# A two-layer MLP behind Nystrom attention: a fourth raw-weight buffer, spills issued by GpSimd, and a rearranged prologue

## The chip, the cores and the metric

One core of a Trainium2 chip. The metric is device time in microseconds (us) of one execution. The page and the trace come from one profiled execution, whose span runs from its first to its last instruction. Engines: PE is TensorE (PEld its weight loads), DVE is VectorE, ACT is ScalarE, POOL is GpSimd, SP is the sync engine, whose queue (SPq) issues all DMAs of the kernel before.

## The reference

Attention over 4 batches, 8 heads, 576 positions, head size 64, with 32 landmarks, then two MLP layers (512 to 2048 to 512) over the 2304 tokens:

```python
q_lm = q.reshape(B, H, m, S // m, D).mean(axis=3)
k_lm = k.reshape(B, H, m, S // m, D).mean(axis=3)
A = sm(q, k_lm); Bm = sm(q_lm, k_lm); C = sm(q_lm, k)
Z = Bm.transpose(0, 1, 3, 2) / (norm1(Bm) * norminf(Bm) + 1e-06)
for _ in range(6):
    Z = 2 * Z - Z @ Bm @ Z
x = (A @ Z @ C @ v)          # heads side by side: 2304 x 512
h = x @ w_in;  x = (h - np.tanh(h)) @ w_out          # first MLP
h = x @ w_in2; out = (h * np.tanh(softplus(h))) @ w_out2   # second MLP
```

## The kernel before

Products are made to float32 accuracy by splitting each operand into a high and a low part (`split`, line 98), three matmuls per product. The weights come from memory as 64-bit values; a load (`load_raw`, line 113) brings 512 KB into a buffer of the pool `raw`, and a conversion (`f32_a`, `f32_b`, lines 124 to 154) makes float32 from it: two ScalarE passes (lines 131 and 137) and a VectorE combination (line 144), after which the buffer is free. Output weights are then split (lines 99 and 100). Input weights of the first MLP are kept whole, two loads side by side in one tile of the pool `w1` (four tiles, `keep_job`, line 163), and spilled to memory once (line 171), to be reloaded for each later batch (line 466). `convert` (line 176) runs a list of such jobs with some loads ahead. In the first batch the list is: four loads for the first of four column blocks of the input weights, nine output weights, then the other column blocks and output weights in the order of their due slots.

The work of the first part is divided into slots. A slot is one of 16 blocks of 128 hidden features for one half (288 positions) of one batch, so there are 32 slots a batch and 128 in all. A slot issues the first-layer matmuls (`h1`, lines 500 to 502, two of each line), the activation (`vec`), and, three slots later, the output matmuls (`y1`, lines 603 to 607). The input weights of a column block are folded with the attention's middle matrix first (`p_gen`, line 468: 16 matmuls on line 211, then the split on lines 479 and 481); slots 0 to 3 need block 0, slots 4 to 7 block 1, and so on. AT, the transposed and split A, comes from `attn_a` (line 409) for each half batch. After slot 127 come 96 slots of the second MLP (lines 524 to 526 and 626 to 631).

The attention of a batch is one serial chain (`attn_pre`, line 240): the means over positions (line 246), scaled copies into QB, KB and behind k (lines 251, 253); the scores of the landmarks against k in two halves, two banks each (line 275, its matmuls on line 211), copied and reduced to maxima (lines 279 to 283); exponentials (lines 293, 296); transposes of C (lines 307, 324) with copies (lines 311, 327); norms of B; C v (lines 351 to 360); B B^T (lines 373 to 375, matmuls on line 218); the iterations (lines 381 to 399); the middle matrix Z0 (lines 400 to 404). A generator yields after each part; a slot, or a round of the prologue, takes the next part of each generator, one in its middle and one at its end.

The prologue (lines 733 to 778) runs the first batch's `attn_pre` at raised priority beside the conversions, and the first half batch's `attn_a`, called the early attention here, from round 8. The order on each engine is laid down when the kernel is built, by priority and readiness in a model; each engine then executes its list in order. The shared PSUM pool `ps_m` has two banks, `ps_h` two, and `ps_y` four, which hold the output sums of `y1`. In the second MLP `convert` uses a second pool of two raw buffers besides `raw`, and `raw` also holds outputs on their way out.

Of the kernel before, what the change touches and what calls it, by code (L numbers as in the profile page):

```python
# [8 lines left out]
F32 = mybir.dt.float32  # L9
# [5 lines left out]
ALU = mybir.AluOpType  # L15
AX = mybir.AxisListType
# [11 lines left out]
def kernel(  # L28
# [11 lines left out]
    nc = tc.nc  # L40
    B, NPAIR, _, S = qT.shape
    NG = NPAIR // 2
# [3 lines left out]
    R = S // M  # L46
# [15 lines left out]
    const = ctx.enter_context(tc.tile_pool(name="const", bufs=1))  # L62
    wo_p = ctx.enter_context(tc.tile_pool(name="wo", bufs=NF))
    st_p = ctx.enter_context(tc.tile_pool(name="st", bufs=4))
    raw_p = ctx.enter_context(tc.tile_pool(name="raw", bufs=3))
    ps_y = ctx.enter_context(tc.tile_pool(name="ps_y", bufs=4, space=PSUM))
    ps_h = ctx.enter_context(tc.tile_pool(name="ps_h", bufs=2, space=PSUM))
    ps_m = ctx.enter_context(tc.tile_pool(name="ps_m", bufs=2, space=PSUM))

    w1s = dram.tile([NG, 4, 128, 2, 512], F32, name="w1s")  # L70
# [15 lines left out]
    V = nc.vector  # L86
    A = nc.scalar
    G = nc.gpsimd
# [24 lines left out]
    def load_raw(src, pool=None):  # L113
        raw = (pool or raw_p).tile([128, 512, 2], U32, tag="raw", name="raw")
        nc.sync.dma_start(out=raw.rearrange("p f t -> p (f t)"), in_=src.bitcast(U32))
        return raw
# [7 lines left out]
    def f32_a(raw, on_act):  # L124


        y = st_p.tile([128, 512], F32, tag="y", name="y")
        hi = raw.bitcast(F32)[:, :, 1]
        one = tables["prelu"]
        if one:  # L130
            A.activation(out=y, in_=hi, func=ACTF.Prelu, scale=2.0 ** -112, alpha=2.0 ** 32)
        else:
            A.activation(out=y, in_=hi, func=ACTF.Copy, scale=2.0 ** -112)
        lo = raw[:, :, 0]
        if on_act:

            A.activation(out=lo, in_=raw.bitcast(U16)[:, :, 1], func=ACTF.Copy, scale=2.0 ** -13,
                         bias=2.0 ** -14 - 0.5)
        else:
            V.tensor_scalar(out=lo, in0=lo, scalar1=29, scalar2=None, op0=ALU.logical_shift_right)  # L140
        return y, lo, one

    def f32_b(y, lo, one, t):
        V.scalar_tensor_tensor(
            out=t.bitcast(U32) if one else lo, in0=y.bitcast(U32), scalar=3, in1=lo,
            op0=ALU.logical_shift_left, op1=ALU.bitwise_or,
        )
        yield 0
        if not one:
            V.scalar_tensor_tensor(  # L150
                out=t.bitcast(U32), in0=y.bitcast(U32), scalar=0x80000000, in1=lo,
                op0=ALU.bitwise_and, op1=ALU.bitwise_or,
            )
            yield 0
# [8 lines left out]
    def keep_job(src, g, j, a):  # L163
        def where():
            if a == 0:
                w1t[0, g, j] = w1_p.tile([128, 2, 512], F32, tag="w1", name="w1")
            return w1t[0, g, j][:, a, :]

        def done(y):
            if a == 1:  # L170
                nc.sync.dma_start(out=w1s[g, j], in_=w1t[0, g, j])
                if g:
                    ready.append(j)
        return src, done, where

    def convert(jobs, act_share=1, more=None):
        n = len(jobs)
        raws, st, los = {}, {}, {}
        ahead = 4 if more else 2

        def fetch(i):
            if i < n:
                raws[i] = load_raw(jobs[i][0], more if more and i % 5 > 2 else None)

        for i in range(ahead):
            fetch(i)
        for i in range(n + 2):
            if i < n:
                st[i], *los[i] = f32_a(raws.pop(i), i % act_share == 0)
            if i - 1 in los:  # L190
                where = jobs[i - 1][2]
                yield from f32_b(st[i - 1], *los.pop(i - 1), where() if where else st[i - 1])
            fetch(i + ahead)
            if i >= 2:
                jobs[i - 2][1](st.pop(i - 2))
            yield 1

    ready = []
    w1t = {}
# [7 lines left out]
    def blocks(outs, lhs, rhs):  # L207
        for c in range(4):
            for e in range(2):
                ps = slice(64 * e, 64 * e + 64)  # L210
                mm(outs[e][32 * c:32 * c + 32], lhs[ps, c, :], rhs(ps, c % 2, c // 2), start=True, stop=True,  # L211
                   tile_position=(64 * e, 32 * c))

    def heads(o, lhs, rhs):

        for c in range(4):
            ps = slice(32 * c, 32 * c + 32)
            mm(o[ps], lhs[ps], rhs[ps], start=True, stop=True, tile_position=(32 * c, 32 * c))

    ATt = {}  # L220
    adone = set()
    ZT = {}

    inp = {}

    def attn_load(b, g):
        r = inp[b, g] = {}
        r["q"] = in_p.tile([128, 2, S], F32, tag="q", name="q")
        r["k"] = in_p.tile([128, 2, S + M], F32, tag="k", name="k")
        nc.sync.dma_start(out=r["k"][:, :, 0:S], in_=kT[b, 2 * g:2 * g + 2].rearrange("a p s -> p a s"))  # L230
        nc.sync.dma_start(out=r["q"], in_=qT[b, 2 * g:2 * g + 2].rearrange("a p s -> p a s"))

    def v_load(b, g):
        t = in_p.tile([128, 5, 256], F32, tag="v", name="v")
        inp[b, g]["v"] = t
        cols = slice(256 * g, 256 * g + 256)
        nc.sync.dma_start(out=t[:, 0:4, :], in_=v[b, 0:512, cols].rearrange("(j p) c -> p j c", p=128))
        nc.sync.dma_start(out=t[0:64, 4, :], in_=v[b, 512:S, cols])

    def attn_pre(b):  # L240
        qs = [inp[b, g]["q"] for g in range(NG)]
        ks = [inp[b, g]["k"] for g in range(NG)]
        red = sm_p.tile([128, NG, 2, 2, M], F32, tag="red", name="red", bufs=1)

        def mean(g, x, t):
            V.tensor_reduce(out=red[:, g, x], in_=t[:, :, 0:S].rearrange("p a (m r) -> p a m r", r=R),
                            axis=AX.X, op=ALU.add)

        def scaled(g, x):
            if x == 0:  # L250
# [20 lines left out]
        for hf in range(2):  # L271
            for g in range(NG):
                inp[b, g]["c"] = c[:, g]
            pp = [ps_m.tile([128, 512], F32, tag="m", name="m") for g in range(NG)]
            blocks([p[:, 0:NH] for p in pp], QB, lambda ps, g, a: ks[g][ps, a, NH * hf:NH * hf + NH])
            yield 1
            n = NH - M * hf
            for g, p in enumerate(pp):
                A.activation(out=c[:, g, NH * hf:NH * hf + NH], in_=p[:, 0:NH], func=ACTF.Copy)
                V.tensor_reduce(out=mx[:, g, hf:hf + 1], in_=p[:, 0:n], axis=AX.X, op=ALU.max)  # L280
                yield 0
                if hf:
                    V.tensor_reduce(out=mx[:, g, 3:4], in_=p[:, n:NH], axis=AX.X, op=ALU.max)
                    yield 0
            yield 1
# [31 lines left out]
        bb = sm_p.tile([128, 2, NG, M], F32, tag="bb", name="bb", bufs=1)  # L317
# [30 lines left out]
                        in1=mask.rearrange("p (o a) m -> p o a m", o=1).to_broadcast([128, NG, 4, M]), op=ALU.mult)  # L348
        yield 1

        pv = ps_m.tile([128, 512], F32, tag="m", name="m")
        for g in range(NG):
            for j in range(5):
                n = 128 if j < 4 else 64
# [14 lines left out]
        for g in range(NG):  # L369
            A.activation(out=yv[:, g, 32:96], in_=pv[:, 64 * g:64 * g + 64], func=ACTF.Copy,  # L370
                         scale=n4[:, 2, g:g + 1])
        yield 1
        py = ps_m.tile([128, 512], F32, tag="m", name="m")
        for g in range(NG):
            heads(py[:, 32 * g:32 * g + 32], bb[:, 1, g, :], bb[:, 1, g, :])
        yield 1
        nr = n4.rearrange("p t (g o) -> p t g o", o=1)[:, 3]
        V.tensor_tensor(out=yv[:, :, 0:32], in0=py[:, 0:64].rearrange("p (g n) -> p g n", g=NG),
# [354 lines left out]
    if True:  # L733
# [4 lines left out]
        def w1i_jobs(j):  # L738
            return [keep_job(w1i[j, g, a], g, j, a) for g in range(NG) for a in range(2)]

        def wo_jobs(src, dst, lo, hi):
            return [split_job(src[i], wo_p, "w", dst, i) for i in range(lo, hi)]

        jobs = w1i_jobs(0) + wo_jobs(w1o, W1o, 0, NPRE)
# [6 lines left out]
        pa = both(attn_a, 0, 0, True)  # L751
        n = nc_ = 0
        live = {"pre": pre, "pa": pa}
        while live or nc_ < PREP:
            st = []
            if "pre" in live:
                st.append("pre")
            if n >= 8 and "pa" in live:
                st.append("pa")
            if n == 1:  # L760
                for g in range(NG):
                    v_load(0, g)
            gens = []
            for k in st:
                if part(live[k]):
                    gens.append(live[k])
                else:
                    del live[k]
            if "pre" not in live and ready and nc_ >= 4 + NPRE - 1:
                pg = p_gen(0, ready.pop(0))  # L770
                part(pg)
                gens.append(pg)
            if (nc_ < 4 + NPRE or (nc_ < PREP and "pre" not in live)):
                part(cv)
                gens.append(cv)
                nc_ += 1
            parts(gens)
            n += 1
# [124 lines left out]
```

## Time and profile before

| | |
|---|---|
| median of 3 runs | 866.72 us (864.64 to 867.72) |
| profiled execution | 864.62 us, its span 862.8 us |
| PE busy | 817.7 us (95%) |
| PEld busy | 708.2 us (82%) |
| DVE, ACT busy | 501.6 us, 497.1 us (58% each) |
| POOL busy | 174.3 us (20%) |
| DMA moved | 79.62 MB, mean 92 GB/s |

Busy shares are means over parts of the kernel with different limits, so they are read by stretch. A wait is idle time of an engine ahead of an instruction, put down to what ended last. The chain of waits is followed back from the last instruction.

### The profile page before, as it was taken

To read this page: it belongs to the slowest core of one execution; us is meant where nothing else is said; L and a number is where in the kernel's file an instruction comes from. 1 tells how busy PE (TensorE), PEld (TensorE's weight loads), DVE (VectorE), ACT (ScalarE), POOL (GpSimd) and SP (SyncE) were. 2 spreads that over 40 slices of the span, in tenths; PEclk is the share of its full clock that TensorE was granted. 3 is DMA by queue.
4 is the path that set the end of the run, shared out by engine and by line. 5 is a ranking of instruction groups with operands and counts; after the bars stand their busy time and mean duration, and the time that the engine had idled before them with its cause. 6 is when DMAs were issued, how large, how long until landed. Compare 5 with 4: busy or idle time off the path is not lost.

```text
span 862.8 us, 14979 instructions
## 1 busy us (share of the span) xinstructions
PE 817.7 (95%) x5656; PEld 708.2 (82%) x5656; DVE 501.6 (58%) x1154; ACT 497.1 (58%) x1234; POOL 174.3 (20%) x202
## 2 busy tenths in 40 slices
PE   3778789999999999999999999999999999999998
PEld 1435579888997899889899989999889999899996
DVE  5787989898879986889992896521111111211111
ACT  4786787788877887789884775333222222222221
POOL 0000000776667855880000000000000000000000
PEclk9998999999999999999999999999999999999999
DMA  8789614151404300153004573021001000100100
GB/s 294 239 271 309 239 51 138 51 181 51 139 1 154 126 2 30 63 182 102 30 1 152 190 220 119 1 64 56 19 1 52 22 1 28 37 1 1 38 1 36
DMA packets 34921, 79.62 MB, mean 92 GB/s; under 512 B 5408, under 2 KB 14112, under 8 KB 34848
## 3 DMA queue, kind: packets, MB, share of 16 engines
q1 hardware_dynamic: 34848, 78.66, 27.7%
q8 instruction: 44, 0.72, 0.3%
q14 instruction: 29, 0.24, 0.1%
HBM read 65.01 MB, written 13.63 MB: 91 GB/s over the span
## 4 chain that ended last, share of the span: by engine, by line
PE 77%; ACT 9%; DVE 7%; POOL 3%; issue 2%; DMA 1%; SPq 0%; DVEq 0%; ACTq 0%; POOLq 0%
PE y L631 7%; PE y L627 7%; PE y L626 7%; PE y L603 6%; PE h L526 5%; PE h L525 5%; PE h L524 5%; PE y L607 5%; PE y L604 5%; PE m L211 4%; PE h L500 3%; PE h L501 3%; PE h L502 3%; PE m L526 2%; PE m L525 2%; PE m L524 2%
## 5 line engine op out<-in xcount | busy, mean ns | idle before, releaser
L574 DVE TENSOR_TENSOR gg<-g,gg 128x384 fp32r<-128x384 f32 x96 | 53.5, 558 | 275.6 <-ACT g L573 275.6
L603 PE MATMUL y<-gg,w 128*128 128x288 f32 x512 | 151.6, 311 | 5.8 <-ACT gg L99 4.2
L604 PE MATMUL y<-gg,w 128*128 128x288 f32 x512 | 143.7, 296 | 0.0
L603 PEld LDWEIGHTS y<-gg,w 128*128 128x128 f32 x512 | 97.0, 189 | 30.7 <-issue 14.8
L607 PE MATMUL y<-gg,w 128*128 128x288 f32 x512 | 110.1, 300 | 1.9 <-DVE gg L100 1.5
L100 POOL TENSOR_TENSOR gg<-g,gg 128x288 fp32r<-128x288 f32 x80 | 69.0, 862 | 206.1 <-ACT gg L99 204.3
L572 ACT ACTIVATE gg<-h 128x384 fp32r<-128x384 f32 x66 | 32.5, 492 | 132.6 <-PE h L526 132.5
L627 PE MATMUL y<-w,gg 128*128 128x512 f32 x256 | 101.2, 395 | 0.0
L626 PE MATMUL y<-w,gg 128*128 128x512 f32 x256 | 100.8, 394 | 0.0
L604 PEld LDWEIGHTS y<-gg,w 128*128 128x128 f32 x512 | 97.3, 190 | 0.8 <-issue 0.8
L631 PE MATMUL y<-w,gg 128*128 128x512 f32 x256 | 88.4, 396 | 0.0
L607 PEld LDWEIGHTS y<-gg,w 128*128 128x128 f32 x512 | 81.7, 190 | 8.1 <-DVE gg L100 3.8
L500 PE MATMUL h<-AT,P 128*128 128x288 f32 x256 | 78.4, 306 | 6.2 <-DVE th L564 4.3
L557 POOL TENSOR_SCALAR mk<-s 128x288 uint8<-128x288 f32 x80 | 77.3, 966 | 7.2 <-ACT s L551 0.7
L502 PE MATMUL h<-AT,P 128*128 128x288 f32 x256 | 77.4, 303 | 0.2 <-DVE P L481 0.2
L501 PE MATMUL h<-AT,P 128*128 128x288 f32 x256 | 77.3, 302 | 0.0
L585 DVE COPY_PREDICATED g<-mk,th 128x288 f32<-128x288 uint8 x128 | 72.8, 569 | 4.6
L99 ACT ACTIVATE gg<-g 128x288 fp32r<-128x288 f32 x128 | 57.0, 445 | 25.0 <-PE y L607 17.3
L567 ACT ACTIVATE q<-q,bias_c 128x288 f32<-128x288 f32 x128 | 69.1, 540 | 2.2
L563 DVE TENSOR_TENSOR g<-h,s 128x288 f32<-128x288 f32 x128 | 57.3, 448 | 21.5 <-ACT th L552 20.9
L551 ACT ACTIVATE s<-h 128x288 f32<-128x288 f32 x128 | 52.4, 410 | 27.2 <-PE h L502 25.8
L572 ACT ACTIVATE gg<-m 128x384 fp32r<-128x384 f32 x30 | 14.8, 492 | 89.3 <-PE m L526 89.3
(154 smaller groups left out, 1858.2 us busy)
## 6 DMA issues: line engine op xcount, KB each, us to landing
w<-w1s SPq DMA_DIRECT2D x24, 512.0 KB, 4.4
raw<-in_w1i_dram SPq DMA_DIRECT2D x16, 512.0 KB, 5.6
raw<-in_w1o_dram SPq DMA_DIRECT2D x16, 512.0 KB, 4.5
raw<-in_w2i_dram SPq DMA_DIRECT2D x16, 512.0 KB, 4.4
raw<-in_w2o_dram SPq DMA_DIRECT2D x16, 512.0 KB, 4.1
k<-in_kT_dram SPq DMA_DIRECT2D x8, 576.0 KB, 6.0
q<-in_qT_dram SPq DMA_DIRECT2D x8, 576.0 KB, 5.8
ys<-raw SPq DMA_DIRECT2D x16, 288.0 KB, 2.3
```

Of the source, the lines that this page charges most:

```text
L500: mm(p, P[:, g, 0, c], AT[:, g, 0, :], start=(g == 0), stop=False)
L501: mm(p, P[:, g, 0, c], AT[:, g, 1, :], start=False, stop=False)
L502: mm(p, P[:, g, 1, c], AT[:, g, 0, :], start=False, stop=(g == NG - 1))
L557: eng.tensor_scalar(out=mk, in0=e, scalar1=FT, scalar2=None, op0=ALU.is_ge)
L567: A.activation(out=q, in_=q, func=ACTF.Square, scale=FB, bias=bias_c[:, 0:1])
L585: V.copy_predicated(out=g0, mask=mk0, data=t0)
L603: mm(yps[d], w[:, 0, c], gg[:, 0, :], start=(f == 0), stop=False)
L604: mm(yps[d], w[:, 1, c], gg[:, 0, :], start=False, stop=False)
L607: mm(yps[d], w[:, 0, c], gg[:, 1, :], start=False, stop=(f == NF - 1))
L626: mm(p, gg[:, 0, cs], w[:, 0, :], start=(f == 0), stop=False)
L627: mm(p, gg[:, 0, cs], w[:, 1, :], start=False, stop=False)
L631: mm(p, gg[:, 1, cs], w[:, 0, :], start=False, stop=(f == NF - 1))
```

## The change

`raw` gets a fourth buffer, and `convert` fetches three loads ahead instead of two; in the second MLP four of six loads go to `raw` instead of three of five. The spills of the input weights are issued by GpSimd instead of SP. For the first batch q and k are loaded in halves (one head pair each) and the means are taken for each half; the second half of the scores goes to two banks of `ps_y`. In every batch B B^T is put ahead of C v. The early attention starts at round 15 instead of 8.

```diff
-    raw_p = ctx.enter_context(tc.tile_pool(name="raw", bufs=3))
+    raw_p = ctx.enter_context(tc.tile_pool(name="raw", bufs=4))
...
             if a == 1:
-                nc.sync.dma_start(out=w1s[g, j], in_=w1t[0, g, j])
+                G.dma_start(out=w1s[g, j], in_=w1t[0, g, j])
...
-        ahead = 4 if more else 2
+        ahead = 4 if more else 3
...
-                raws[i] = load_raw(jobs[i][0], more if more and i % 5 > 2 else None)
+                raws[i] = load_raw(jobs[i][0], more if more and i % 6 > 3 else None)
...
-        nc.sync.dma_start(out=r["k"][:, :, 0:S], in_=kT[b, 2 * g:2 * g + 2].rearrange("a p s -> p a s"))
-        nc.sync.dma_start(out=r["q"], in_=qT[b, 2 * g:2 * g + 2].rearrange("a p s -> p a s"))
+        for t, src in ((r["k"], kT), (r["q"], qT)):
+            if b:
+                nc.sync.dma_start(out=t[:, :, 0:S], in_=src[b, 2 * g:2 * g + 2].rearrange("a p s -> p a s"))
+            else:
+                for a in range(2):
+                    nc.sync.dma_start(out=t[:, a, 0:S], in_=src[b, 2 * g + a])
...
-            V.tensor_reduce(out=red[:, g, x], in_=t[:, :, 0:S].rearrange("p a (m r) -> p a m r", r=R),
-                            axis=AX.X, op=ALU.add)
+            if b:
+                V.tensor_reduce(out=red[:, g, x], in_=t[:, :, 0:S].rearrange("p a (m r) -> p a m r", r=R),
+                                axis=AX.X, op=ALU.add)
+            else:
+                for a in range(2):
+                    V.tensor_reduce(out=red[:, g, x, a], in_=t[:, a, 0:S].rearrange("p (m r) -> p m r", r=R),
+                                    axis=AX.X, op=ALU.add)
...
-            pp = [ps_m.tile([128, 512], F32, tag="m", name="m") for g in range(NG)]
+            if b == 0 and hf:
+                pp = [ps_y.tile([128, 512], F32, tag="y", name="y") for g in range(NG)]
+            else:
+                pp = [ps_m.tile([128, 512], F32, tag="m", name="m") for g in range(NG)]
...
+        py = ps_m.tile([128, 512], F32, tag="m", name="m")
+        for g in range(NG):
+            heads(py[:, 32 * g:32 * g + 32], bb[:, 1, g, :], bb[:, 1, g, :])
+        yield 1
         pv = ps_m.tile([128, 512], F32, tag="m", name="m")
...
-        yield 1
-        py = ps_m.tile([128, 512], F32, tag="m", name="m")
-        for g in range(NG):
-            heads(py[:, 32 * g:32 * g + 32], bb[:, 1, g, :], bb[:, 1, g, :])
         yield 1
...
-            if n >= 8 and "pa" in live:
+            if n >= 15 and "pa" in live:
```

## Rows read from the trace of the kernel before

**Rows 1.** Windows by stage: busy us of PE, PEld, DVE, ACT, POOL; clock, DMA, GB/s

```profile
0.00:43.75 43.75, 24.30 (x270) 11.52 (x271) 28.13 (x73) 25.91 (x60) 0.68 (x6) 1.00 0.79 266
43.75:59.70 15.95, 11.98 (x46) 5.38 (x46) 13.55 (x29) 13.00 (x31) 0.00 (x0) 1.00 0.84 270
...
66.30:73.20 6.90, 6.90 (x21) 3.54 (x23) 6.23 (x19) 4.69 (x11) 0.00 (x0) 0.51 0.92 314
...
103.90:107.30 3.40, 3.40 (x20) 2.15 (x21) 3.40 (x10) 2.18 (x7) 0.00 (x0) 0.50 0.98 399
...
640.00:680.00 40.00, 40.00 (x203) 36.15 (x202) 7.09 (x14) 11.94 (x27) 0.00 (x0) 1.00 0.14 40
```

**Rows 2.** Windows with line 500 alone, two matmuls a slot: busy PE, PEld

```profile
43.70:63.60 19.90, 3.68 (x8) 2.27 (x8) 1.00 0.85 272
63.60:125.55 61.95, 7.72 (x24) 4.50 (x24) 0.92 0.62 214
125.55:174.86 49.31, 9.54 (x32) 6.15 (x33) 1.00 0.25 83
```

**Rows 3.** Chain that ended last, 0 to 50 us: start, us, what

```profile
2.22 7.33 DMA q<-in_qT_dram
...
9.57 1.36 DVE red L246
...
11.27 1.25 PE m L211 x12
12.52 1.05 PE h L211 x12
...
14.90 1.73 PE m L211 x16
...
21.58 0.49 ACT s L437 x2
...
23.81 0.86 PE m L358 x22
...
29.05 1.78 PE m L358 x44
...
43.75 0.61 PE h L500
```

**Rows 4.** PE's timeline from 24.6 us; then the chain in the next batch

```profile
24.60 0.31 PE L218 MATMUL m<-bb 32*32 32x32 f32 x2
24.84 0.42 PE L358 MATMUL m<-v,k 128*32 128x64 f32 x2
25.20 0.31 PE L218 MATMUL m<-bb 32*32 32x32 f32 x2
...
127.41 1.66 PE m L358 x80
```

**Rows 5.** PE's timeline in the iterations; the last step of AT, by tile

```profile
34.28 0.86 PE L218 MATMUL m<-yv 32*32 32x96 f32 x16 [0.48 <-DVE yv L387]
...
L100 DVE TENSOR_TENSOR AT<-th,AT x2: 448/450/451, 30.2 to 34.7; 128x288 fp32r<-128x288 f32 x2
```

**Rows 6.** Timelines of SP and ACT, 48 to 60 us; SP's waits to 126 us

```profile
48.52 0.67 ACT L131 ACTIVATE y<-raw 128x512 f32<-128x512 f32 x1
...
53.68 0.33 SPq L115 DMA_DIRECT2D raw<-in_w1i_dram  x1
...
58.98 0.65 ACT L131 ACTIVATE y<-raw 128x512 f32<-128x512 f32 x1
...
SPq L115 <- DVE w L144: 31.2, 13, 7.6
```

**Rows 7.** Page part 6 for the spills (us to landing last); timelines of SP, DVE

```profile
w1s<-w SPq DMA_DIRECT2D x8, 512.0 KB, 6.3
...
58.34 0.43 SPq L171 DMA_DIRECT2D w1s<-w  x1
...
78.43 0.69 DVE L144 SCALAR_TENSOR_TENSOR w<-y,raw 128x512 uint32<-128x512 uint32 x1 [5.33 <-ACT raw L137]
```

More of the change, by code (lines that the diff above doesn't have):

```diff
@@ L221 @@
     adone = set()
-    ZT = {}
     inp = {}
```

## The prediction

> **What bounds the kernel now.** First, the windows by stage [rows 1]. From 640 to 680 us TensorE is busy in all 40.00 of 40.00 us, and, its own weight loads aside, no engine in a third of it: the long second part is a row of matmuls, and nothing outside TensorE is worth anything there. Before that, the first 43.75 us hold 24.30 us of TensorE work, and from 43.75 to 59.70 us ScalarE is busy in 13.00 of 15.95 us, VectorE in 13.55 and the DMA engines in 0.84.
>
> Second, the pace of the slots, counted by the first-layer matmuls, two a slot [rows 2]. Slots 0 to 3 take 19.90 us, slots 4 to 15 take 61.95 us, slots 16 to 31 take 49.31 us. So a slot costs 3.08 us once the kernel runs smoothly, and 5.1 us over the first sixteen (81.85 / 16). Two sums can be shortened, the 43.75 us before slot 0 and the 32.6 us (81.85 - 16 x 3.08) that slots 0 to 15 lose. What is won there shifts all that follows, since TensorE is full behind it.
>
> Third, the chain that ended last, from 0 to 44 us [rows 3]. The reader is to see one serial chain: the last q load lands at 9.55, its mean takes 1.36 us, the first half of the scores begins at 11.27, the early attention's own matmuls stand in it for 1.05 us, the second half begins only at 14.90, an exponential of the early attention stands in it for 0.49 us, C v begins at 23.81 and its last piece at 29.05 (1.78 us, to 30.83), and the first h1 matmul is at 43.75.
>
> **The change, part by part.**
>
> *Halved loads and means, first batch.* Four loads become eight and four means become eight of half the width. The chain waits for the last mean: half of 1.36 is 0.68, so **-0.7 us**. The cost is four more issues on SP at 0.33 to 0.43 us [rows 6], 1.3 to 1.7 us by which the weight and v loads behind them are issued later. The cover is the q and k traffic itself, which lands until 9.55; those loads are behind it anyway. Without that cover it would cost up to 1.7 us.
>
> *Two more banks for the second half of the scores, and the early attention put off to round 15.* The second half waits from the end of the first (12.52) to 14.90, for its banks; with banks of its own it can follow at once, 2.4 us sooner. The early attention's 1.05 us may still be put between, since its inputs are ready first: then 1.3. I take **-2.0**. The 0.49 us of its exponential may go as well or be replaced by a weight conversion (0 to -0.5): **-0.2**. What is late next is the two maxima on VectorE, as now.
>
> *B B^T ahead of C v.* Now both are issued alternately: two matmuls of C v, two of B B^T. A pair of pairs takes 0.60 us (24.60 to 25.20) [rows 4], eight of them 4.8, while 44 matmuls of C v alone take 1.78 us, 0.04 us each. Between 23.81 and 30.83, 7.0 us pass. Apart they would be 80 x 0.04 = 3.2 us and, for the 16 of B B^T, the 0.86 us that 16 matmuls of such tiles take in an iteration [rows 5], together 4.1: **-2.9**. If B B^T goes while TensorE waits for the transposed C, -3.8; if the order stays mixed, 0. The new wait is for a bank: B B^T holds one of the two shared banks until it is scaled, so C v has only the other. In the later batches C v is already unmixed, 80 matmuls in 1.66 us of the chain [rows 4]; the swap costs and gives nothing there, hidden in a full TensorE.
>
> *The early attention beside the iterations.* What leaves the chain above runs later. The iterations leave little room: 16 matmuls of 0.86 us after a wait of 0.48 for VectorE [rows 5]; each of the six can be pushed by one foreign VectorE instruction, such as the 0.45 us of AT's subtraction [rows 5]. Bounds 0 and +2.7, I take **+0.5**, near the present rows, where such work is already mixed in.
>
> Sum up to the first h1: -0.7 - 2.0 - 0.2 - 2.9 + 0.5 = **-5.3 us**, 38.4 instead of 43.75.
>
> *Fourth buffer, three loads ahead.* Slot 4 needs the second column block of the input weights. Its last load is issued at 53.68, after a wait for the buffer, and converted at 58.98 [rows 6]: 5.3 us from issue to use, three buffers, so a conversion about every 2.5 us. SP's waits for VectorE's conversions sum to 31.2 us in 13 waits on this line alone [rows 6]. With a fourth buffer the load can go one conversion earlier. But ScalarE has only 2.95 us free in this stretch (15.95 - 13.00), which bounds the gain: 0 to -2.95, I take **-1.5**. A load more stands ahead of v in the first 10 us; v has until C v, now at 23.81, then near 21 us. The rearranged loads of the second part (four of six in this pool) lie beside a TensorE that is always busy: nothing.
>
> *Spills from GpSimd's queue.* Eight issues of 0.43 us leave SP [rows 6, 7]; GpSimd is busy for 0.68 us in the first 43.75 and not at all in the later stretches of rows 1. No row shows a store that GpSimd issues. Below: it saves 8 x 0.43 = 3.4 us of SP's time, which is worth nothing where SP waits for buffers. Above: a spill must end before its tile is written again. The third is issued at 58.34, lands 6.3 us later, and its tile's slot is wanted again at 78.43 [rows 7]: 13.8 us of slack. I take **0**, nearest to the landing shown.
>
> The Trainium skill, page "SBUF — State Buffer", section "SBUF: two separate sides", speaks against this part: a DMA issued by GpSimd needs descriptors that GpSimd itself writes, and it is locked out while VectorE runs a copy or scalar operation that uses both ports; the page gives 3.1 us instead of 0.62 for one such DMA. By it a spill would be up to 2.5 us later (an estimate from that page), and the sum would stay as it is.
>
> All: -5.3 - 1.5 = -6.8 us. The profiled execution took 864.62 us (its span 862.8), which becomes 857.8; it lies 2.1 us under the median of 866.72, so for the median **860 us** (866.72 - 6.8 = 859.9). Its own range, from the bounds: -0.7 - 2.4 - 0.5 - 3.8 - 2.95 = -10.3 us to -0.7 - 1.3 + 2.7 = +0.7, or 856.4 to 867.4; I count as the forecast what lies under 864.
>
> **The rivals.**
>
> *The whole start runs denser.* Slots 4 to 15 lose 25 us (61.95 - 12 x 3.08), and TensorE's granted clock was at half, 1.2 GHz, for 6.9 us from 66.30 and 3.4 us from 103.90 [rows 1], up to 5.2 us of it. If earlier conversions close some of these stalls, and the clock stays at 2.4 GHz, the gain is 5.2 more and perhaps a third of the other 20: 847 to 856. Against: the order on each engine is laid down beforehand, and a stall may just move. Chance 0.20.
>
> *The gain is given back.* The DMA engines are already busy at 0.79, 0.84 and 0.92 of the time up to 73 us [rows 1]. If the loads can't come faster, the first h1 is early and slot 4 is where it was; 0 to 2.5 us remain: 864 to 867. Chance 0.12.
>
> *Slower: the early attention comes too late.* It must give AT before the first h1. Now AT is finished at 35.2 (the last at 34.7 and 0.45) [rows 5], 8.5 us ahead; with lower priority it competes with thirteen rounds of conversions. It decides when AT comes after 38.4. If it waits for all of them, the thirteenth starting at 48.52 [rows 6], the first h1 is at about 50, 6 us later than now: 868 to 873. Against: it was also run in gaps before. Chance 0.08.
>
> *Slower: stores starve.* From 13.8 us beyond today's landing [rows 7], VectorE stops at the reuse of a spill's tile, with all conversions and slots queued behind it; the gain is gone at 13.8 + 6.8 = 20.6 us, and 2 to 4 us beyond that give 868 to 871. The Trainium skill's page "SBUF — State Buffer", named above, has the mechanism. Against: GpSimd has nothing else to do there, and the delay would have to be over three times the 6.3 us that a spill takes to land. Chance 0.04.
>
> **How the numbers follow.** The forecast has 0.56, the denser start 0.20, the given-back gain 0.12, the two slower ones 0.12. About 0.3%, 2.6 us, is what a measurement of this kernel can tell from no change: faster 0.76, same 0.12, slower 0.12. The range of 848 to 869 takes the forecast, nearly all of the denser start, the given-back gain and the nearest part of the slower ones; the open ends of these stretches keep it at 8 in 10.
>
> **What would show it.** Right: the second half of the scores follows the first at once; B B^T stands as one block of 16 and C v as 80 without mixing; the first h1 is near 38.4; the load for the second column block is issued one conversion earlier; slot 16 starts near 119 instead of 125.6, and from there all is as before. Wrong: h1 waits for AT; VectorE waits for a store; the first h1 early but slot 16 at 125; or slot 16 before 113, which would be the denser start.

## The result, and the profile after

| | before | after |
|---|---|---|
| median of 4 runs each | 867.22 us (864.64 to 868.38) | 852.18 us (851.32 to 852.99) |
| profiled execution, its span | 864.62, 862.8 us | 851.59, 849.8 us |

The ratio is 0.983, 95% interval 0.9805 to 0.9856: 15 us faster, where 7 were forecast. The sign was right and the time lies in the range, but the time is that of a rival, the denser start. (One of the four executions of the run with three buffers again, below, took 4338.66 us and is left out of its numbers.)

First the pace of the slots of the kernel after. The h1 matmuls now stand on lines 511 to 513. The columns are the window, its length, busy PE, PEld, granted clock, DMA share, GB/s, for line 511 alone; these rows answer to [rows 2].

```profile
40.30:61.00 20.70, 4.20 (x8) 2.47 (x8) 0.55 0.89 325
61.00:113.00 52.00, 7.65 (x24) 4.75 (x24) 0.90 0.58 214
113.00:162.20 49.20, 9.61 (x32) 6.09 (x33) 1.00 0.25 83
```

Slots 0 to 3 take 20.70 us (19.90 before), slots 4 to 15 take 52.00 (61.95), slots 16 to 31 take 49.20 (49.31). So of 13.0 us of span, 3.4 come ahead of slot 0 and about 10 from slots 4 to 15; slot 16 starts at 113.06 instead of 125.58, and nothing behind it changed: slots 32 and 96 start 12.6 us earlier too.

Next the same stretches with all engines (busy PE, PEld, DVE, ACT, POOL; clock, DMA, GB/s), first of before, then of after.

```profile
43.75:63.60 19.85, 15.82 (x68) 7.97 (x68) 16.96 (x36) 16.01 (x37) 0.00 (x0) 1.00 0.85 272
63.60:125.55 61.95, 50.30 (x289) 34.68 (x290) 50.77 (x123) 48.32 (x120) 0.00 (x0) 0.92 0.62 214
```

```profile
40.30:61.00 20.70, 19.32 (x68) 9.56 (x68) 15.98 (x37) 17.35 (x37) 2.24 (x4) 0.55 0.89 325
61.00:113.00 52.00, 46.53 (x289) 33.50 (x290) 48.95 (x119) 44.51 (x115) 1.06 (x2) 0.90 0.58 214
```

The reader is to see that slots 4 to 15 hold nearly the same work, about 50 us of VectorE, in 10 us less. VectorE was busy 82% of the time (50.77 of 61.95) and is now at 94% (48.95 of 52.00), ScalarE went from 78% to 86%. What went is idle time, and the waits name it. Before, 43.75 to 126 us (engine, line, what it waited for: us in total, times, longest):

```profile
DVE w L144 <- ACT raw L137: 8.1, 6, 5.3
...
ACT P L479 <- PE m L211: 6.8, 3, 5.1
...
PE m L211 <- DVE w L144: 4.9, 2, 4.0
```

After, 40.3 to 113 us, where the copies of P stand on lines 490 and 492:

```profile
POOL w1s L171 <- DVE w L144: 40.9, 5, 23.4
...
PE h L511 <- ACT P L490: 5.1, 2, 3.7
...
ACT P L490 <- PE m L211: 1.9, 1, 1.9
...
DVE w L144 <- ACT raw L137: 0.3, 1, 0.3
```

Before, VectorE stood 8.1 us for ScalarE's half of a conversion, TensorE stood for the converted weights of a fold, and ScalarE for the fold. After, the first is 0.3 us, the second is gone and the third is 1.9. What rose is TensorE's wait for the copy of P at the start of a slot, 5.1 us against 1.7. GpSimd's 40.9 us cost nothing: up to slot 16 its queue has nothing but the spills. The conversions themselves show the same: before, the one at 58.98 was the 17th, and the 25th began at 90.78; now they begin at 46.55 and 66.84.

Then the prologue, as the chain of waits of after, which answers to [rows 3].

```profile
1.63 4.37 DMA q<-in_qT_dram
...
6.79 2.25 DVE red L254 x3
9.04 1.51 DVE red L254 x2
...
10.57 0.27 ACT qb L261
...
10.88 0.74 PE m L211 x5
...
24.42 0.32 ACT yv L385
...
28.24 4.86 DMA raw<-in_w1o_dram
...
33.18 0.68 ACT y L131
```

From 6.79 to 10.55 the halved means stand back to back, so VectorE, not the load, now sets the scores' start. At the end of the chain no attention stands: ScalarE takes up a conversion whose weight has just landed. TensorE's timeline for C v, which answers to [rows 4]:

```profile
20.76 0.44 PE L218 MATMUL m<-bb 32*32 32x32 f32 x16
21.53 2.83 PE L373 MATMUL m<-v,k 128*32 128x64 f32 x80 [0.33 <-ACT k L338]
```

B B^T is one block of 16 and C v one of 80, as forecast. Z0 is copied at 34.32 instead of 40.23, but the first h1 starts at 40.33, 3.4 us earlier, not 5.9. ScalarE's timeline shows where the rest stayed:

```profile
34.32 0.25 ACT L415 ACTIVATE z<-m 128x128 f32<-128x128 f32 x1
...
35.00 0.66 ACT L131 ACTIVATE y<-raw 128x512 f32<-128x512 f32 x1
...
36.64 0.65 ACT L131 ACTIVATE y<-raw 128x512 f32<-128x512 f32 x1
...
38.27 0.65 ACT L131 ACTIVATE y<-raw 128x512 f32<-128x512 f32 x1
...
39.37 0.42 ACT L99 ACTIVATE AT<-th 128x288 fp32r<-128x288 f32 x1
39.70 0.57 ACT L490 ACTIVATE P<-m 128x512 fp32r<-128x512 f32 x1
```

The fold's matmuls are done by about 36.6 (from 34.63, 1.96 us). The copy of P that h1 needs is laid down behind three conversions and AT's own copy, and starts at 39.70, 3.1 us after its matmuls are done.

Last the spills, which answer to [rows 7], in the profile page's list of issues:

```profile
w1s<-w POOLq DMA_DIRECT2D x8, 512.0 KB, 6.9
```

They land 6.9 us after their issue, against 6.3 from SP before. With the spills put back on SP and all else as after (a run below) they land in 6.9 as well, so GpSimd's queue adds nothing that shows. A GpSimd issue takes 0.53 to 0.77 us, one on SP before 0.42 to 0.43. The Trainium skill's page "SBUF — State Buffer", section "SBUF: two separate sides", warns that VectorE can lock GpSimd out, so that it cannot write the descriptors of a DMA that it issues. No row here shows that, beside a VectorE that is busy for most of the time; which of its instructions would lock GpSimd out, no run tells.

### The profile page after: what moved, and what is told of

Its sections match the earlier page's. It is cut to its first block, busy times and chain, and to the rows that moved or that the text cites. A ratio compares the mean times of both kernels' runs of the same rounds, so it can differ in the third digit from the quotient of the medians.

```text
span 849.8 us, 15003 instructions
## 1 busy us (share of the span) xinstructions
PE 812.7 (96%) x5656; PEld 706.5 (83%) x5656; DVE 503.3 (59%) x1158; ACT 496.6 (58%) x1234; POOL 179.0 (21%) x210
## 4 chain that ended last, share of the span: by engine, by line
PE 74%; DVE 12%; ACT 5%; POOL 3%; DMA 2%; issue 2%; SPq 0%; DVEq 0%; ACTq 0%
PE y L642 7%; PE y L638 7%; PE y L637 7%; PE y L614 6%; PE h L537 5%; PE h L536 5%; PE h L535 5%; PE y L618 5%; PE y L615 5%; PE m L211 3%; PE m L537 2%; PE h L511 2%; PE m L536 2%; PE m L535 2%; DVE g L596 2%; PE h L513 2%
## 5 line engine op out<-in xcount | busy, mean ns | idle before, releaser
L562 ACT ACTIVATE s<-h 128x288 f32<-128x288 f32 x128 | 52.6, 411 | 23.9 <-PE h L513 23.8
```

## The experiments

Ratios are to the kernel before, measured beside it, with a 95% interval; us are medians, and a second figure behind "against" is that of the kernel before. Positions of slots, conversions and Z0 are from each kernel's profiled execution.

### Each part alone on the kernel before

**The fourth buffer with its fetch depth**

```diff
-    raw_p = ctx.enter_context(tc.tile_pool(name="raw", bufs=3))
+    raw_p = ctx.enter_context(tc.tile_pool(name="raw", bufs=4))
...
-        ahead = 4 if more else 2
+        ahead = 4 if more else 3
...
-                raws[i] = load_raw(jobs[i][0], more if more and i % 5 > 2 else None)
+                raws[i] = load_raw(jobs[i][0], more if more and i % 6 > 3 else None)
```

> The kernel before with the fourth raw buffer, three loads ahead and the four-of-six rule alone. Theory of the buffers (the gain of slots 4 to 15 comes from conversions that start earlier because SP no longer waits for a buffer): 856 to 860 us against 867, the first h1 still near 43.7 us, and slots 4 to 15 in about 53 us instead of 62. Rival, the prologue (an earlier start carries all of it): 866 to 868. Rival, the spills on SP hold the loads back, so buffers alone do little: 863 to 867.

855.93 against 865.47, ratio 0.9883 [0.9846, 0.9921]: 9.5 us, at the lower edge of the theory of the buffers. Its two stretches, slots 0 to 3 and 4 to 15, in windows with all engines:

```profile
43.45:64.05 20.60, 15.29 (x68) 7.76 (x68) 18.85 (x43) 19.92 (x42) 0.00 (x0) 1.00 0.92 319
64.05:115.90 51.85, 43.33 (x289) 34.39 (x290) 48.61 (x117) 44.62 (x115) 0.00 (x0) 0.90 0.64 235
```

Slot 4 is where it was (64.08; 63.62 before) and slot 16 comes at 115.93. In slots 0 to 3 ScalarE fills up (19.92 of 20.60 us) with conversions that used to come later: 42 instructions instead of 37. Slots 4 to 15 reap it, with 115 ScalarE instructions instead of 120 in 51.85 us.

**The buffer without the depth** (bufs=4 alone)

> The kernel before with the fourth raw buffer alone: still two loads ahead, still three of five in the second MLP. If the buffer itself is what counts: 855 to 858, as the run with all three. If the three loads ahead are needed for it: 862 to 867.

855.54 against 865.37, ratio 0.9875 [0.9839, 0.9910]. The whole gain is the buffer's, as the first expectation had it. The depth does move conversions: the 23rd starts at 66.40 (65.97 with the depth, 79.11 before), but the 25th only at 80.63 (70.83 with it). Slot 16 comes at 115.63 all the same, so the 25th alone is no sign of the time.

**The spills' queue**

```diff
-                nc.sync.dma_start(out=w1s[g, j], in_=w1t[0, g, j])
+                G.dma_start(out=w1s[g, j], in_=w1t[0, g, j])
```

> The kernel before with the spills issued by GpSimd alone. Theory of the buffers: 866 to 868 us, no change, since no wait of SP was put down to a spill. Rival of the spills: 858 to 863, with earlier loads in 40 to 100 us. Rival of the prologue: 867.

859.91, ratio 0.9929 [0.9904, 0.9954]: 5.6 us faster alone. Slot 0 came later (47.37; ScalarE stood for raw loads of 6.68 and 5.66 us in the chain), slots 4 to 15 took 55.55 us instead of 61.95, and the 25th conversion starts at 82.60 instead of 90.78. The time and the earlier conversions are those of the spills' rival; the theory of the buffers, no change, missed.

**The prologue** (the rest of the diff of the change, from the halved loads on: halves, banks, B B^T first, round 15)

> The kernel before with the halved loads and means, the two more banks, B B^T ahead of C v and the early attention from round 15, and nothing else. Theory of the buffers: the first h1 at 40 to 41 us and about 863 us, 3 to 4 less than before; slots 4 to 15 still take about 62 us. Rival of the prologue: 852 to 855.

857.22, ratio 0.9897 [0.9856, 0.9939]: 8.2 us, between the two expectations. In the profiled execution slot 0 starts at 37.35, 6.4 us earlier, Z0 comes at 34.32, and slots 4 to 15 still take 63.0 us: what the prologue wins there is won ahead of slot 0, and part of it is lost behind. That execution was the longest of the four (861.35; the others 855.04 to 858.36), and how the others ran through slots 4 to 15 is not known.

**The late start of the early attention**

```diff
-            if n >= 8 and "pa" in live:
+            if n >= 15 and "pa" in live:
```

> The kernel before with the early attention from round 15 alone. It takes nothing away and adds nothing, only an order. If order alone moves this kernel by several us, so that the 5.6 us of the spills alone may be order: 860 to 864 or 868 to 872. If it doesn't: 865 to 868, and the spills' 5.6 us need another cause.

866.55 against 865.72, ratio 1.0007 [0.9987, 1.0027]. It was also meant to test whether any reshuffled order explains the 5.6 us of the spills. In its trace up to 130 us a single ScalarE instruction stands in another place than before, so for that it is weak; the cause of the 5.6 us stays open. That raw loads queue on SP behind a spill that waits for its conversion fits, but was only argued.

### One part taken back from the kernel after

**Three buffers again** (the first diff, reversed)

> The changed kernel with three raw buffers, two loads ahead and three of five again. Theory of the buffers: 861 to 864 us, slots 4 to 15 back at about 62 us. Rival of the prologue or of the spills: 852 to 855, as the changed kernel.

853.80, ratio 0.9872 [0.9823, 0.9922], from executions of 859.43 (the profiled one), 853.80 and 853.39 us. The theory's 861 to 864 was missed, and the median is in the rival's range. Slot 0 stays (40.03), and the stretches of the profiled execution are:

```profile
40.00:60.55 20.55, 16.07 (x68) 9.31 (x68) 15.90 (x35) 17.20 (x37) 1.07 (x2) 0.61 0.83 289
60.55:120.35 59.80, 50.15 (x289) 35.18 (x290) 49.74 (x124) 48.68 (x122) 2.13 (x4) 0.89 0.57 206
```

Here slots 4 to 15 are back at 59.80 us, and the 25th conversion starts at 82.05, not 66.84; of the two shorter executions no rows are known. As the last of the edits the buffer is worth 1.6 us by the medians, 3.6 by the ratios, whose intervals overlap, and 7.8 by the profiled executions (859.43 and 851.59); alone it was 9.5. So this run leaves its price beside the other two parts open.

**Spills on SP again** (the line of the spills' diff, reversed)

> The changed kernel with the spills on SP's queue again. Theory (with a fourth buffer SP's queue is not what loads wait for): 851 to 854 us, no change. Rival (the spills on SP's queue hold back loads, as the run with the spills alone on GpSimd suggests with its 5.6 us): 856 to 859.

850.70, ratio 0.9817 [0.9793, 0.9841], 1.5 us under the kernel after and within the intervals, as the theory had it. With four buffers the queue of the spills is worth nothing that can be measured, one way or the other. This is also the buffer and the prologue without the spills: 6.9 us below the prologue alone by the ratios (0.9897) and 5.7 below the buffer alone (0.9883), and neither pair of intervals overlaps. Slot 0 starts at 38.35.

**B B^T behind C v again**

```diff
-        py = ps_m.tile([128, 512], F32, tag="m", name="m")
-        for g in range(NG):
-            heads(py[:, 32 * g:32 * g + 32], bb[:, 1, g, :], bb[:, 1, g, :])
-        yield 1
         pv = ps_m.tile([128, 512], F32, tag="m", name="m")
...
+        py = ps_m.tile([128, 512], F32, tag="m", name="m")
+        for g in range(NG):
+            heads(py[:, 32 * g:32 * g + 32], bb[:, 1, g, :], bb[:, 1, g, :])
+        yield 1
```

> The changed kernel with B B^T behind C v again. Theory (the mixing of the two kinds of matmul is what the reordering takes away, 2.9 us, and the first h1 carries it): yv 2.5 to 3.5 us later than the 24.4 of the changed kernel and 854 to 856 us against 852. Rival (what is won before the first h1 is lost behind it, at the low clock of TensorE or in ScalarE's queue): yv later as well, but 851 to 853.

855.02 against 865.37, ratio 0.9867 [0.9829, 0.9904]; yv (the scaled C v) at 27.62 instead of 24.42, Z0 at 38.85, slot 0 at 44.89. The theory held at yv and in the median; the interval overlaps that of the kernel after. The mixing is back on TensorE's timeline:

```profile
23.00 0.42 PE L370 MATMUL m<-v,k 128*32 128x64 f32 x2
23.36 0.31 PE L218 MATMUL m<-bb 32*32 32x32 f32 x2
23.60 0.42 PE L370 MATMUL m<-v,k 128*32 128x64 f32 x2
...
25.38 2.18 PE L370 MATMUL m<-v,k 128*32 128x64 f32 x52
```

**The second half of the scores in the shared banks again**

```diff
-            if b == 0 and hf:
-                pp = [ps_y.tile([128, 512], F32, tag="y", name="y") for g in range(NG)]
-            else:
-                pp = [ps_m.tile([128, 512], F32, tag="m", name="m") for g in range(NG)]
+            pp = [ps_m.tile([128, 512], F32, tag="m", name="m") for g in range(NG)]
```

> The changed kernel with the second half of the scores in the shared banks again. Theory: the second half of the scores waits for the maxima again, the exponentials about 2 us later, 853 to 855. Rival (lost behind the first h1 anyway): 851 to 853.

851.83, ratio 0.9831 [0.9789, 0.9874]. Z0 comes 2.3 us later (36.59), slot 0 only 0.5 us (40.83) and the end not at all, as the rival had it: the fold is done at 38.88 and P's copy starts at 40.19, so it waits 1.3 us for ScalarE's list where it waits 3.1 in the kernel after.

**Whole loads and means again**

```diff
-        for t, src in ((r["k"], kT), (r["q"], qT)):
...
-                for a in range(2):
-                    nc.sync.dma_start(out=t[:, a, 0:S], in_=src[b, 2 * g + a])
+        nc.sync.dma_start(out=r["k"][:, :, 0:S], in_=kT[b, 2 * g:2 * g + 2].rearrange("a p s -> p a s"))
+        nc.sync.dma_start(out=r["q"], in_=qT[b, 2 * g:2 * g + 2].rearrange("a p s -> p a s"))
...
-                for a in range(2):
-                    V.tensor_reduce(out=red[:, g, x, a], in_=t[:, a, 0:S].rearrange("p (m r) -> p m r", r=R),
...
+            V.tensor_reduce(out=red[:, g, x], in_=t[:, :, 0:S].rearrange("p a (m r) -> p a m r", r=R),
...
```

> The changed kernel with whole q and k loads and whole means in the first batch. Theory: the scores start 0.6 to 0.7 us later and 852 to 853.5, at the edge of what can be told. Rival (fewer issues on SP are worth as much as the shorter mean): 851 to 852.

849.53, ratio 0.9809 [0.9772, 0.9846], under both ranges; 2.7 us under the kernel after by the medians, with intervals that overlap. The scores start at 11.47 instead of 10.88, 0.6 us later, as the theory had it, but Z0 comes at 33.98 instead of 34.32: the halves gain 0.6 us at the scores and nothing from Z0 on. Slot 16 comes at 109.66 instead of 113.06; why, is open. The means of q in this kernel, then in the kernel after, on VectorE up to 12 us (count, then busy us and mean ns, then idle us before); those of k take the same each:

```profile
L246 DVE TENSOR_REDUCE red<-q 128x64 f32<-128x1152 f32 x2 | 2.7, 1352 | 0.3
```

```profile
L254 DVE TENSOR_REDUCE red<-q 128x32 f32<-128x576 f32 x4 | 3.0, 753 | 1.0 <-DMA q<-in_qT_dram 1.0
```

A half mean costs 753 ns, not 676, which is half of 1352: eight take 6.0 us, four whole ones 5.4.

**Round 8 again**

```diff
-            if n >= 15 and "pa" in live:
+            if n >= 8 and "pa" in live:
```

> The changed kernel with the early attention from round 8 again. Theory (the late start of the early attention cost part of the gain: in the changed kernel AT ended at 40.6 us and the folded weights' copy waited behind it, though Z0 was ready at 34.3): the first h1 near 37.5 instead of 40.3, and 849 to 852 us against 852. Rival (the late start keeps its instructions out of the score chain, and gives more than it costs): Z0 later by 1 to 2 us and 853 to 856.

851.30, ratio 0.9815 [0.9789, 0.9842]: the theory's time, but not its path. Z0 comes at 36.89, 2.6 us later, which is the rival's sign, and slot 0 at 41.28 rather than near 37.5. The last step of AT starts at 41.06 (40.11 in the kernel after), so the round is not what sets AT's time.

### The clock, and a version that goes further

**Filler matmuls.** Thirteen matmuls into a bank that nobody reads: one in each of five iterations, eight behind the matmuls of the first fold.

```diff
...
+    def warm(rhs, n):
+        if not wt:
+            wt.append(ps_y.tile([128, 512], F32, tag="y", name="y"))
+        for _ in range(n):
+            mm(wt[0][:, 0:rhs.shape[1]], ident, rhs, start=True, stop=True)
...
+            if b == 0:
+                warm(yv[:, 0], 1)
...
+        if b == 0 and j == 0:
+            warm(Z0.rearrange("p c m -> p (c m)"), 8)
```

> The changed kernel with 13 added matmuls that nothing reads: one behind each of five iterations and eight between the folding of the first block and the first h1. It tells what the low clock of TensorE costs the early slots (slots 0 to 4 take 20.7 us in the changed kernel, with TensorE busy in 19.3 of 19.7 us at half clock from 40.3 to 60). If the clock rises earlier through it and TensorE is the bound there: slots 0 to 4 in 14 to 17 us and 846 to 850. If ScalarE and VectorE are the bound: slots 0 to 4 unchanged at about 20, and 851 to 854.

853.17, ratio 0.9841 [0.9818, 0.9863]. First the two stretches of the kernel after at the lower clock, then windows of the one with fillers:

```profile
18.20:59.20 41.00, 31.89 (x288) 16.50 (x287) 34.29 (x86) 35.34 (x75) 2.25 (x4) 0.50 0.86 304
62.50:72.70 10.20, 10.20 (x34) 4.41 (x34) 8.35 (x24) 7.58 (x18) 0.53 (x1) 0.51 1.05 396
```

```profile
38.20:51.80 13.60, 10.28 (x59) 4.87 (x61) 11.61 (x25) 12.40 (x26) 1.18 (x2) 0.99 0.95 331
51.80:72.30 20.50, 17.51 (x60) 9.37 (x53) 16.00 (x42) 15.99 (x37) 1.59 (x3) 0.51 1.03 386
```

In the kernel after the clock is at half, 1.2 GHz, for 51 us of the start. With fillers it is full in 38.2 to 51.8 and falls again. Slot 2 comes 2.5 us earlier, slot 4 only 0.7, slot 16 0.4, and the end none: a full clock for those 13.6 us is worth nothing at the end, as the second expectation had it. What a full clock in the whole start would be worth, no run shows.

**A fifth buffer in the first batch**, from a pool that is free only then

```diff
-    def convert(jobs, act_share=1, more=None):
+    def convert(jobs, act_share=1, more=None, k=6):
...
-                raws[i] = load_raw(jobs[i][0], more if more and i % 6 > 3 else None)
+                raws[i] = load_raw(jobs[i][0], more if more and i % k > 3 else None)
...
-        cv = vec_only(convert(jobs), rate)
+        raw3 = att.enter_context(tc.tile_pool(name="raw3", bufs=1, side="right"))
+        cv = vec_only(convert(jobs, 1, raw3, 5), rate)
```

> The changed kernel with a fifth raw buffer and four loads ahead in the first batch. If the number of buffers still bounds the conversions: the 25th conversion before 64 us (66.8 in the changed kernel) and 846 to 850. If the DMA engines, busy at 0.88 and 1.03 from 40 to 80 us, or ScalarE are the bound now: 851 to 854.

848.27, ratio 0.9787 [0.9764, 0.9809]: 3 to 4 us more, as the first expectation had it, though the intervals just overlap. Slot 4 comes at 57.63 (61.03), slot 16 at 110.86, the 25th conversion at 62.20. So the gain is ahead of slot 4; slots 4 to 15 take 53.2 us, against 52.0 with four buffers.

**P's copy ahead of the conversions**

```diff
-                pg = p_gen(0, ready.pop(0))
+                pg = hi(p_gen(0, ready.pop(0)), 60)
```

> The changed kernel with raised priority for the folding of the first column block in the prologue. If the folded weights' copy, queued behind conversions and AT on ScalarE, is what keeps the first h1 at 40.3 us: the copy at 36.5 to 37.5, and, if the early slots then carry it, 848 to 851; if ScalarE's and VectorE's work or the low clock bounds the early slots, 851 to 853.

850.66, ratio 0.9814 [0.9790, 0.9838]. P's copy starts at 37.36 and slot 0 at 38.01, 2.3 us earlier; slot 16 is 1.8 earlier, and the end 1.5 by the medians, within the intervals. The queue ahead of P's copy is what held the first h1, as the first expectation had it. Behind it AT is the next wait: its second copy starts only at 41.12, and the matmuls of slots 0 and 1 that need it at 41.62.

**Combinations.** Five buffers with the spills on SP and the whole prologue; the same with whole loads; and five buffers, whole loads and P's copy first, with the spills on GpSimd and on SP.

> The changed kernel with a fifth raw buffer and four loads ahead in the first batch, and the spills on SP again. If the buffers are still the bound and the spills' queue is worth nothing: 846 to 849 us. If the spills on GpSimd are needed for it: 850 to 853.

> The fifth buffer, spills on SP, whole q and k loads and whole means, the banks, B B^T first and the early attention from round 15. If whole loads are as good as halves or better (849.5 against 852.2 us in the changed kernel): 845 to 848. If that difference was order alone: 847 to 851.

> The changed kernel with a fifth raw buffer in the first batch, whole q and k loads and means, and raised priority for the first folding. If these are separate causes: 843 to 847 us. If they all close the same stalls of the slots 4 to 15: 847 to 850.

> The same with the spills on SP. If the spills' queue is worth nothing once the buffers are there: within 2 us of the run before it. If it is worth something: 3 us or more slower.

| kernel | us | ratio [95%] | slot 0 | slot 16 |
|---|---|---|---|---|
| five, spills SP, halves | 849.81 | 0.9798 [0.9768, 0.9828] | 37.09 | 113.38 |
| five, spills SP, whole loads | 848.22 | 0.9790 [0.9759, 0.9820] | 37.16 | 110.21 |
| five, whole, P first, spills GpSimd | 848.47 | 0.9824 [0.9799, 0.9850] | 37.23 | 109.47 |
| five, whole, P first, spills SP | 848.26 | 0.9831 [0.9794, 0.9868] | 36.93 | 108.62 |

All end at 848.2 to 849.8, 2 to 4 us under the kernel after, so single gains no longer add up: the third is in the range of one shared cause (847 to 850), and the fourth within 2 us of it, so the spills' queue is worth nothing there either. The first falls between its two ranges: with the spills on SP five buffers are 0.9 us by the medians under four (850.70), within the intervals. The second is in the range of order alone (847 to 851), only 0.2 us above the other. The third's stretches (slots 0 to 3, then 4 to 15, all engines):

```profile
37.20:57.30 20.10, 16.06 (x68) 7.85 (x68) 19.02 (x43) 20.02 (x43) 2.13 (x4) 1.00 0.92 319
57.30:109.45 52.15, 45.55 (x290) 35.03 (x291) 48.81 (x118) 44.72 (x115) 1.07 (x2) 0.87 0.59 225
```

ScalarE is busy for 20.02 of 20.10 us, then VectorE for 48.81 of 52.15. So the start looks bounded by the work of these two, conversions above all; no run takes work off them, so this is not shown.

## Why the prediction was right or wrong

**The fourth buffer: the step that failed.** It was put at -1.5 and bounded at -2.95 by ScalarE's free time in one stretch, 43.75 to 59.70 us, as if slot 4 alone waited. But the same wait for a buffer stood ahead of the later conversions too. SP's waits of the kernel before, 40 to 126 us (line, what it waited for: us in total, times, longest):

```profile
SPq L115 <- DVE w L144: 26.2, 11, 7.6
SPq L115 <- DVE y L144: 18.7, 8, 3.7
```

Alone the buffer gave 9.5 and 9.8 us, and none of it at slot 4: all between slots 4 and 16, in which ScalarE had 13.6 us free before (61.95 - 48.32). On top of the prologue it gave 6.9. In the profiled executions slots 4 to 15 take 55.5 to 63.0 us in all five kernels with three buffers (before, and four runs) and 49.6 to 53.6 in all fifteen with four or five; the 23rd conversion starts at 76.65 to 79.22 us in the five and at 58.27 to 67.75 in the fifteen. This bears out the wait for a buffer as the mechanism; what stays open is its price beside both other parts, 1.6 to 7.8 us. The prediction's own row of the pace held the loss of 25 us in slots 4 to 15; it was given to a rival at 0.20 instead of to the term. A load took 5.3 us from issue to use [rows 6], and with more buffers more loads are under way in that time. A fifth buffer does not shorten slots 4 to 15 any more.

**The prologue: right in sum, handed over in part.** Its -5.3 is near the 5.7 us that it gave on top of the buffer, with the spills on SP; alone it gave 8.2. Up to Z0 it gave -5.9, but the first h1 came at 40.33, not 38.4. Missing in the sum was what stands between Z0 and h1 on ScalarE: conversions laid down ahead of P's copy. The run with that copy first shows it (37.36 instead of 39.70). How long the copy waits there differs from kernel to kernel: 0.1 us with the prologue alone, where slot 0 starts at 37.35, and 1.0 with the spills on SP, where it starts at 38.35.

Term by term, each taken back from the kernel after: B B^T ahead of C v -2.9 forecast, 3.2 us at yv and 4.5 at Z0; the banks -2.0, 2.3 at Z0 and nothing at the end; halved loads -0.7, 0.6 at the scores and nothing from Z0 on; the early attention's later start +0.5, 0.6 at Z0 alone on the kernel before (40.84 against 40.23), but 2.6 the other way in this company. These do not add up to 5.9: terms that are taken back one by one cannot be summed. The rival of the late attention came about in its place though not in its effect: the last step of AT came at 40.1, after the 38.4 from which it was to decide, but AT's copy stood directly ahead of P's, so it cost at most its own 0.4 us. With P's copy first, AT does become the wait.

**Spills: 0 was right in this company**, and not alone, where they gave 5.6 us. Alone the three parts gave 9.5, 8.2 and 5.6, together 15.0 and not 23.3. What is counted twice is above all the spills: without them buffer and prologue together give as much (850.70 us). That spills and buffer relieve the same queue of loads fits, but was only argued. The rival of starving stores didn't come about: the spills land 0.6 us later than before, and it was to decide at 20.6.

**The denser start** had its mechanism named rightly (earlier conversions close stalls), and the time lies in its range; its sign, slot 16 before 113, was missed by 0.06 us (113.06). But nearly half its price (5.2 of 12 us) was put on TensorE's clock, and the clock gave little back: of its two stretches at 1.2 GHz the first is there after as well (62.5 to 72.7 us, against 66.3 to 73.2), and the second, 3.4 us, is gone, which by the clock alone is worth at most half of it, 1.7 (an estimate). In the clock column the kernel after is even at half for longer, 51 us against 10. But the spacing of the matmuls shows the same slow pace in both starts (last section), so that difference is not one of pace, and the 1.00 of [rows 1] up to 59.70 us does not show a fast one. Fillers that raised the clock gave nothing at the end. **The second part** stayed as it was: slots 16 to 31 take 49.20 us against 49.31.

## What to carry to other kernels

When a wait for a buffer recurs at each step of a pipeline, its cost is to be summed over all the stretches in which the consumers have idle time, not over the one where it is first met. What an edit wins on a serial chain is handed on only if the next engine's list, laid down in advance, has that work next; look at what the consumer's engine executes just ahead of it. Gains of parts need not add up, so a part is judged alone, taken back, and in pairs with the others.

## What was not expected of the hardware

Alternating between the two kinds of small matmuls is dear: a pair of pairs takes 0.60 us in the run with B B^T behind C v, and 0.40 in the kernel with the spills moved alone:

```profile
25.09 0.24 PE L218 MATMUL m<-bb 32*32 32x32 f32 x2
25.26 0.30 PE L358 MATMUL m<-v,k 128*32 128x64 f32 x2
25.49 0.24 PE L218 MATMUL m<-bb 32*32 32x32 f32 x2
...
27.67 1.51 PE L358 MATMUL m<-v,k 64*32 64x64 f32 x44
```

Unmixed, 44 of them take 1.51 us, 0.034 each. Why the mixed price differs is not shown. It may be the clock: in the run with the spills alone the granted clock is 1.00 from 23.8 to 27.6 us. In the run with B B^T behind C v the column says 1.00 as well, but 16 matmuls of an iteration right behind take 0.86 us, as they do at 0.50 in the kernel after, and not 0.53 as in the later batches at 1.00.

So the clock column doesn't tell all. In the kernel before it reads 1.00 from 43.75 to 59.70 us, while matmuls of 288 columns follow each other there at 0.24 us, as in the kernel after at 0.50, and at 0.13 from 60 us on:

```profile
56.25 0.44 PE L502 MATMUL h<-AT,P 128*128 128x288 f32 x1
56.49 0.44 PE L500 MATMUL h<-AT,P 128*128 128x288 f32 x1
...
60.22 0.29 PE L500 MATMUL h<-AT,P 128*128 128x288 f32 x1
60.35 0.29 PE L501 MATMUL h<-AT,P 128*128 128x288 f32 x1
```
